# Top-k attention and two mixtures: how the first row tile passes the first mixture

## The chip, the cores and the metric

The kernel runs on one core of a Trainium2 chip. The metric is the device time of one execution in microseconds (us); three runs of the kernel before took 1279.56, 1282.32 and 1282.41 us, a median of 1282.32.

## The reference, cut to what matters

```python
# attention: 2 batches, 8 heads, 576 tokens, head size 64
scores = q @ k^T / 8
kth = the 32nd largest score of each row
attn = softmax(where(scores >= kth, scores, -1e9))
x = (attn @ v), heads side by side            # 1152 rows x 512
# first mixture: 512 -> 2048 -> 512
h = x @ w_in
x = (h * sigmoid(h)) @ w_out
# second mixture: 8 experts, 512 -> 1024 -> 512, Sinkhorn-normalised gates P (1152 x 8)
for e in range(8):
    out += P[:, e:e+1] * (maximum(x @ w1[e], 0) @ w2[e])
```

All inputs are drawn in double precision; `w_in` and `w_out` (and the other arrays) lie in DRAM as 8-byte words where they are double, and the kernel makes 4-byte floats of `w_in` and `w_out` itself.

## The kernel before, in words

The 1152 rows of x are nine row tiles of 128. Row tile 0 alone is group 0; tiles 1 and 2, 3 and 4, 5 and 6, 7 and 8 are groups 1 to 4. A group's attention is done in four units, one for each pair of heads; the unit of head pair p makes the 128 columns of chunk p of x. A score tile is 128 rows of scores against 576 keys: TensorE multiplies (L296), ScalarE copies the scores out of PSUM (L299), VectorE finds the 32 largest by four MAX8 and three MATCH_REPLACE (L308, L314), ScalarE takes the exponential (L312), VectorE masks and sums (L317), GpSimd adds 1e-9 (L319), VectorE takes the reciprocal (L320), ScalarE scales (L321), TensorE turns the tile (L324, L326), ScalarE copies it out (L337, L338), and TensorE multiplies by v into `pav` (L334). For group 0 the result goes into `x0` (L373).

Row tile 0 goes on first (`row_ffn` with the name m0, L497): for each of four column blocks F of 512 hidden columns, four products with the chunks of x0 (L515) into `banks[2]`, a tanh on ScalarE (L523), a multiply on VectorE that makes `gr` (L524), four turns (L531), a copy (L534), and, one block later, four products with `w_out` (L505) into `banks[0]`. Each 32-bit product of 128 by 512 columns shows as two records in the trace. The result becomes row tile 0 of `x1` (`x1_tile`, L584 to L593), and from there TensorE has other work than attention at any time: row tile 0 of experts 0 to 5 (`FILL`), then group 1's first mixture, and so on.

`w_in` and `w_out` come as 32 blocks of 128 by 512 double words (`first_blocks`, L454). Each block is loaded (L473) and narrowed (`narrow`, L439): ScalarE makes the upper bits (L445), GpSimd a correction `cv_n` from the lower word (L448), VectorE joins them (L452). The raw blocks rotate through four buffers, `cv_n` through five. The order of the blocks is by F: four of `w_in`, then four of `w_out`, four times. After the last load the 32 narrowed blocks are written to DRAM (L480) for the later groups.

The keys of a pair of heads are split into an upper and a lower part before they are turned: ScalarE copies (L214), GpSimd subtracts (L215), TensorE turns both (L219, L223), ScalarE copies out (L220, L225). All turns of keys and queries share one PSUM buffer.

Each engine runs its instructions in one order, which a scheduler writes when the program is built. It is steered by `tc.cur_priority`: lower numbers go first. All DMAs are issued by SyncE (SP), one after the other; where one has to wait, those behind it wait too.

Of the kernel before, what the change touches and what calls it, by code (L numbers as in the profile page):

```python
# [35 lines left out]
CVN = 5  # L36
# [12 lines left out]
NATURAL = True  # L49
EARLY_W = 0  # L50


def conv_at(i):

    return 11 * GAP + i * GAP * 2 // 32

# [8 lines left out]
def topk_attention_moe_sinkhorn_kernel(  # L65
# [128 lines left out]
    def load_kv(b, p):  # L194
        kn = nat.tile([P, 5, 2, 1 + NATURAL, D], F32, name=f"kn_{b}_{p}", tag="kn")
        vn = kvp.tile([P, 2, 5, D], F32, name=f"vn_{b}_{p}", tag="vn")
        ks, vs = (x[b, 2 * p : 2 * p + 2] for x in (k, v))
        for j in range(2):
            nc.sync.dma_start(kn[:, 0:4, j, 0, :], ks[j, 0 : 4 * P, :].rearrange("(p c) d -> p c d", c=4))
        nc.sync.dma_start(kn[0:64, 4, :, 0, :], ks[:, 4 * P : S, :].rearrange("h p d -> p h d"))  # L200
# [5 lines left out]
        return kn, vn  # L206

    def turn_kv(b, p, kn, vn):

        kk = kvp.tile([P, 2, S], F32R, name=f"kk_{b}_{p}", tag="kk")  # L210
        if NATURAL:
# [16 lines left out]
        def evac(cols, ps):  # L228
            for j in range(2):
                r, o = (slice(i * 64, (i + 1) * 64) for i in (j, 1 - j))  # L230
                nc.scalar.activation(kk[r, j, cols], ps[r], AF.Copy)
                nc.vector.tensor_sub(kk[o, j, cols], ps[r], kk[r, j, cols].bitcast(F32))

        pk = ps_p.tile([P, 4, P], F32, name=f"pk_{b}_{p}", tag="pp")
        for c in range(4):
            nc.tensor.transpose(pk[:, c, :], kn[:, c, :, 0, :].rearrange("p h d -> p (h d)"), ident)
        evac(slice(0, 512), pk.rearrange("p c t -> p (c t)"))
        pk2 = ps_p.tile([P, 64], F32, name=f"pk2_{b}_{p}", tag="pp")
        nc.tensor.transpose(pk2, kn[0:64, 4, :, 0, :].rearrange("p h d -> p (h d)"), ident[0:64, 0:64])
        evac(slice(512, S), pk2)  # L240
# [14 lines left out]
    def turn_q(b, p, t0, n, half, qn):  # L255
# [14 lines left out]
        pq = ps_p.tile([P, 2, 2 * P], F32, name=f"pq_{b}_{p}_{t0}", tag="pp")  # L270
# [18 lines left out]
    def score_tile(nm, qq, qL, kk, heads, cols):  # L289
# [29 lines left out]
        tiny.tensor_scalar(sm[:, 2:3], sm[:, 1:2], 1e-9, None, op0=ALU.add)  # L319
# [24 lines left out]
    def load(unit):  # L344
        g, p, b, t0, n, half, o = unit
        new = (b, p) not in kv
        if new:
            kv[b, p] = load_kv(b, p)
        return new, load_q(b, p, t0, n, half)

    def turn(unit, got):
        g, p, b, t0, n, half, o = unit
        if got[0]:
            kv[b, p] = turn_kv(b, p, *kv[b, p])
        return turn_q(b, p, t0, n, half, got[1])
# [83 lines left out]
    def narrow(x, src, i):  # L439
# [8 lines left out]
        nc.gpsimd.tensor_scalar(n, lo.bitcast(U32), 2.0**-32 * 7.49, None, op0=ALU.mult)  # L448
# [5 lines left out]
    def first_blocks():  # L454
# [5 lines left out]
        for i in (*range(15, nb), *reversed(range(15))):  # L460
            got[i] = cvp.tile([P, W], F32, name=f"wf_{i}", tag=f"wf{i}", bufs=1)
        for i in range(nb):
            tc.cur_priority = conv_at(i)
            F, part, c = i // (2 * NDC), i // NDC % 2, i % NDC
            r = slice(c * P, (c + 1) * P) if part == 0 else slice((F * NDC + c) * P, (F * NDC + c + 1) * P)
            cols = slice(F * W, (F + 1) * W) if part == 0 else slice(0, W)
            x = got[i]
            if w_in.dtype == F32:
                loaded = nc.sync.dma_start(x, (w_in, w_out)[part][r, cols])
            else:  # L470
                raw = cvp.tile([P, W], w_in.dtype, name=f"wfr_{i}", tag="raw")
                tc.cur_priority = 0 if i < EARLY_W else conv_at(i)
                loaded = (nc.scalar if i < EARLY_W else nc.sync).dma_start(raw, (w_in, w_out)[part][r, cols])  # L473
# [7 lines left out]
        return lambda F: [[got[(2 * F + part) * NDC + c] for c in range(NDC)] for part in range(2)]  # L481
# [15 lines left out]
    def row_ffn(nm, xF, y, gT_ps, blocks, nF, silu, pool):  # L497
# [10 lines left out]
        for F in range(nF):  # L508
            a, b = blocks(F)
            ph = banks[2]  # L510
            for c in range(NDC):
                if type(xF) is tuple:
                    mm3(ph, xF[0][:, c, :], xF[1][:, c, :], a[c][:, 0:W], a[c][:, W:], c == 0, c == NDC - 1)
                else:
                    nc.tensor.matmul(ph, xF[:, c, :], a[c], start=c == 0, stop=c == NDC - 1)  # L515
            kept = tc.cur_priority
            tc.cur_priority = uid() * 100
            g = x1p.tile([P, W], F32, name=f"gr_{nm}_{F}", tag="x1") if silu and NATURAL else \
                pool.tile([P, W], F32, name=f"gr_{nm}_{F}", tag="g")
            if silu:  # L520

                t = pool.tile([P, W], F32, name=f"tr_{nm}_{F}", tag="t")
                nc.scalar.activation(t, ph, AF.Tanh, scale=0.5)  # L523
                nc.vector.scalar_tensor_tensor(g, t, 1.0, ph, op0=ALU.add, op1=ALU.mult)  # L524
            else:
                nc.scalar.activation(g, ph, AF.Relu)
# [118 lines left out]
    qs = turn(units[0], got[0])  # L645
    for u, unit in enumerate(units):
# [19 lines left out]
        if g == 0:  # L666
# [3 lines left out]
            row_ffn("m0", x0, banks[0], banks[1], blocks, DFF // W, True, hp0)  # L670
# [343 lines left out]
```

## Time and profile before

| | us |
|---|---|
| median of three runs | 1282.32 |
| the profiled execution | 1280.4 |
| its span, first to last instruction | 1278.5 |
| TensorE busy | 1201.5 (94%) |
| VectorE busy | 815.7 (64%) |

The page's slices show VectorE at nine tenths or more from the second slice to the fifteenth (a slice is 32 us), and TensorE at nine tenths or more from the sixth to the end, after 4, 5, 6 and 8 tenths. To read the profile: a stretch of the span is taken by itself, the engine that is never idle in it is looked up, and then what the other engines wait for there. The row "TensorE's clock" (PEclk) is the granted share of 2.4 GHz; 0.50 is 1.2 GHz.

### The profile page before, as it was taken

The numbers are of one execution on the slowest core, as the hardware profiler recorded it, in microseconds if no ns is written. First come the engines' busy times: TensorE is split into PE (matmuls) and PEld (weight loads), VectorE is DVE, ScalarE is ACT, GpSimd is POOL, SyncE is SP. The second block draws the span as 40 slices with busy tenths as digits, with TensorE's granted clock in tenths as the row PEclk, the third lists the DMA queues.
The fourth block names the chain that finished last, engine by engine and source line by source line (L and its number), as shares of the span: only waits on it lengthen the run. The fifth ranks groups of instructions, "written<-read, shape, count | busy, mean of one in ns | idle before, by whom it ended". The sixth has DMA issues, their size and how long they took to land.

```text
span 1278.5 us, 17534 instructions
## 1 busy us (share of the span) xinstructions
PE 1201.5 (94%) x6035; PEld 950.3 (74%) x6035; DVE 815.7 (64%) x1531; ACT 580.8 (45%) x1132; POOL 572.8 (45%) x645
## 2 busy tenths in 40 slices
PE   4568999999999999999898999999999999999998
PEld 3444666678767778888676888888888888888887
DVE  4999999989999999132455543454534445354343
ACT  5665777777776577322312332232332322233221
POOL 7971476767751274220233443353444433344310
PEclk9868999999999999999998999999999999999999
DMA  8776576799867689775432312131121111211001
GB/s 235 224 240 226 177 238 221 251 351 323 291 231 246 216 298 326 248 248 181 154 110 82 91 50 66 34 91 42 34 73 43 58 46 45 66 36 56 25 1 66
DMA packets 126538, 193.07 MB, mean 151 GB/s; under 512 B 22896, under 2 KB 68976, under 8 KB 126448
## 3 DMA queue, kind: packets, MB, share of 16 engines
q1 hardware_dynamic: 126448, 191.94, 45.8%
q8 instruction: 48, 0.79, 0.3%
q14 instruction: 42, 0.34, 0.1%
HBM read 152.85 MB, written 39.06 MB: 150 GB/s over the span
## 4 chain that ended last, share of the span: by engine, by line
PE 68%; DVE 25%; DMA 2%; ACT 2%; issue 1%; POOL 1%; DVEq 0%; SPq 0%; POOLq 0%; ACTq 0%
DVE m L308 9%; PE h L140 9%; PE h L138 9%; PE h L139 8%; DVE w L314 7%; PE yA L140 4%; PE yA L139 4%; PE yA L138 4%; PE yB L138 4%; PE yB L139 4%; PE yB L140 4%; DVE s L317 3%; PE bank L138 3%; PE bank L139 3%; PE bank L140 3%; PE bank L505 2%
## 5 line engine op out<-in xcount | busy, mean ns | idle before, releaser
L130 POOL TENSOR_TENSOR wp<-rw,wp 128x512 fp32r<-128x512 f32 (+1 forms) x56 | 86.7, 1571 | 207.8 <-ACT wp L129 207.8
L308 DVE MAX8 m<-w 128x8 f32<-128x576 f32 x192 | 139.3, 743 | 0.3
L130 POOL TENSOR_TENSOR wa<-raw,wa 128x512 fp32r<-128x512 f32 x88 | 116.7, 1337 | 36.3 <-ACT wa L129 29.1
L130 POOL TENSOR_TENSOR w<-rw,w 128x512 fp32r<-128x512 f32 x56 | 73.1, 1308 | 107.4 <-ACT w L129 107.4
L314 DVE MATCH_REPLACE8 w<-m,w 128x576 f32<-128x576 f32 x128 | 94.3, 738 | 0.0
L138 PE MATMUL yB<-w,gH_0b 128*128 128x512 f32 x208 | 81.0, 390 | 0.0
L139 PE MATMUL yB<-w,gH_0b 128*128 128x512 f32 x208 | 81.0, 389 | 0.0
L865 DVE SCALAR_TENSOR_TENSOR gL_0b<-gB,gH_0b 128x512 fp32r<-128x512 f32 (+1 forms) x56 | 45.0, 803 | 55.3 <-ACT gH_0b L864 54.5
L140 PE MATMUL yB<-w,gL_0b 128*128 128x512 f32 x208 | 80.2, 390 | 0.0
L317 DVE SCALAR_TENSOR_TENSOR s<-s,m,e 128x576 f32<-128x576 f32 x64 | 68.9, 1077 | 0.3
L864 ACT ACTIVATE gH_0b<-gB 128x512 fp32r<-128x512 f32 (+1 forms) x56 | 33.6, 600 | 76.5 <-PE yB L139 43.5
L138 PE MATMUL h<-x1H,wp 128*128 128x512 f32 x168 | 67.0, 399 | 0.1
L140 PE MATMUL h<-x1H,wp 128*128 128x512 f32 x168 | 67.0, 399 | 0.0
L139 PE MATMUL h<-x1L,wp 128*128 128x512 f32 x168 | 66.8, 397 | 0.0
L321 ACT ACTIVATE s<-s,sm 128x576 f32<-128x576 f32 x64 | 49.7, 779 | 32.0 <-DVE sm L320 31.6
L312 ACT ACTIVATE e<-s,sm 128x576 f32<-128x576 f32 x64 | 50.0, 781 | 30.1 <-DVE s L317 18.6
L878 DVE TENSOR_TENSOR gB<-u,h 128x512 f32<-128x512 f32 x56 | 38.5, 688 | 37.4 <-PE h L140 37.3
L129 ACT ACTIVATE w<-rw 128x512 fp32r<-128x512 f32 x56 | 34.7, 627 | 58.9 <-PE yB L140 45.7
L505 PE MATMUL bank<-wb,gT_e 128*128 128x512 f32 x128 | 58.8, 599 | 1.7 <-ACT gT_e L534 1.7
L130 DVE TENSOR_TENSOR wp<-sp,wp 128x1024 fp32r<-128x1024 f32 x28 | 44.7, 1596 | 20.2 <-ACT wp L129 20.2
L324 PE MATMUL pt<-ident,s 128*128 128x128 f32 x256 | 43.6, 297 | 13.6 <-ACT s L321 12.7
L334 PE MATMUL pav<-aT,vn 128*64 128x256 f32 (+3 forms) x480 | 53.3, 354 | 2.9 <-ACT aT L337 2.5
(348 smaller groups left out, 3645.6 us busy)
## 6 DMA issues: line engine op xcount, KB each, us to landing
rw<-in_moe_w_dram SPq DMA_DIRECT2D x112, 256.0 KB, 2.7
wa<-sk SPq DMA_DIRECT2D x48, 512.0 KB, 4.1
wb<-sk SPq DMA_DIRECT2D x48, 512.0 KB, 4.3
raw<-in_moe_w_dram SPq DMA_DIRECT2D x80, 256.0 KB, 4.1
wb<-in_moe_w_dram SPq DMA_DIRECT2D x32, 512.0 KB, 5.2
sk<-wa SPq DMA_DIRECT2D x24, 512.0 KB, 4.2
sk<-wb SPq DMA_DIRECT2D x24, 512.0 KB, 4.2
wfr<-in_moe_w_in_dram SPq DMA_DIRECT2D x16, 512.0 KB, 4.6
```

The source lines that it names most:

```text
L130: eng.tensor_sub(dL, src, dH.bitcast(F32))
L138: nc.tensor.matmul(ps, wH, xH, start=first, stop=False, skip_group_check=more)
L139: nc.tensor.matmul(ps, wH, xL, start=False, stop=False, skip_group_check=more)
L140: nc.tensor.matmul(ps, wL, xH, start=False, stop=last, skip_group_check=more)
L308: nc.vector.max(mr, src)
L312: nc.scalar.activation(e, s, AF.Exp, scale=SCALE, bias=sm[:, 0:1])
L314: nc.vector.match_replace(out=w, in_to_replace=mr, in_values=src, imm_value=-3e38)
L317: nc.vector.scalar_tensor_tensor(s, s, m8[:, TOPK - 1 : TOPK], e, op0=ALU.is_ge, op1=ALU.mult, accum_out=sm[:, 1:2])
L321: nc.scalar.activation(s, s, AF.Copy, scale=sm[:, 3:4])
L334: nc.tensor.matmul(ps[r, :n], vn[:, j, c, :], aT[j][:, c, :n], start=c == 0, stop=c == 4)
L505: nc.tensor.matmul(y, gT[:, c * P : (c + 1) * P], b[c], start=F == 0 and c == 0, stop=F == nF - 1 and c == NDC - 1)
L865: nc.vector.scalar_tensor_tensor(gL, src, 0.0, gH.bitcast(F32), op0=ALU.max, op1=ALU.subtract)
```

## The change

Five things change.

1. In `first_row`, which takes the place of `row_ffn` for row tile 0 of the first mixture, blocks F = 0, 1 and 2 are summed side by side in three PSUM banks, one product for each as soon as a chunk of x0 is there. F = 3 follows when bank 2 is free. Turns and second products come after.
2. The 32 blocks are narrowed in another order: all 16 of `w_in` by chunk, then the 16 of `w_out`. The first six raw loads get an earlier priority.
3. Every third `cv_n` is made by ScalarE in place of GpSimd; `cv_n` has four buffers in place of five.
4. The first unit's keys are turned as they are; upper and lower part are made when they leave PSUM, by ScalarE and VectorE (what the code had under `NATURAL = False`), and the first unit's turns use free banks in place of the shared buffer.
5. The loads of v get a later priority than those of k and q.

```diff
-CVN = 5
+CVN = 4
...
-NATURAL = True
-EARLY_W = 0
+V_LATE = GAP
+SOON = 6
+ON_ACT = 3
...
-        def evac(cols, ps):
-            for j in range(2):
-                r, o = (slice(i * 64, (i + 1) * 64) for i in (j, 1 - j))
-                nc.scalar.activation(kk[r, j, cols], ps[r], AF.Copy)
-                nc.vector.tensor_sub(kk[o, j, cols], ps[r], kk[r, j, cols].bitcast(F32))
+        def evac(j, cols, ps):
+            r, o = (slice(i * 64, (i + 1) * 64) for i in (j, 1 - j))
+            nc.scalar.activation(kk[r, j, cols], ps[r], AF.Copy)
+            nc.vector.tensor_sub(kk[o, j, cols], ps[r], kk[r, j, cols].bitcast(F32))
...
+        pk2 = banks[0][:, 0:64]
+        nc.tensor.transpose(pk2, kn[0:64, 4, 0, :, :].rearrange("p h d -> p (h d)"), ident[0:64, 0:64])
...
+        pq = banks[1].rearrange("p (a b) -> p a b", a=2) if first else \
+            ps_p.tile([P, 2, 2 * P], F32, name=f"pq_{b}_{p}_{t0}", tag="pp")
...
+        if new:
+            kept = tc.cur_priority
+            tc.cur_priority += V_LATE
+            load_v(b, p, kv[b, p][1])
+            tc.cur_priority = kept
...
-        nc.gpsimd.tensor_scalar(n, lo.bitcast(U32), 2.0**-32 * 7.49, None, op0=ALU.mult)
+        if ON_ACT and i % ON_ACT == ON_ACT - 1:
+            nc.scalar.activation(n, lo.bitcast(U32), AF.Copy, scale=2.0**-32 * 7.49)
+        else:
+            nc.gpsimd.tensor_scalar(n, lo.bitcast(U32), 2.0**-32 * 7.49, None, op0=ALU.mult)
...
+        order = [(0, F, c) for c in range(NDC) for F in range(DFF // W)] + \
+            [(1, F, c) for F in range(DFF // W) for c in range(NDC)]
...
+    def first_row(xF, got, pool):
...
+        y, gT_ps = banks[0], banks[1]
+        ph = [banks[2], banks[1], banks[0]] + [banks[2]] * (nF - 3)
...
+        for c in range(NDC):
+            for F in range(3):
+                hide(F, c)
+        silu(0)
+        silu(1)
+        turned(0)
+        silu(2)
+        for F in range(3, nF):
+            for c in range(NDC):
+                hide(F, c)
+            turned(1)
+            silu(F)
+        for F in range(nF):
+            second(F)
+            if F + 2 < nF:
+                turned(F + 2)
```

TensorE at the start of the program, before: `pk` are turned keys, `pq` turned queries, `ps` scores; names end with unit and tile.

```order
L219 MATMUL pk_0_0_156<-ident,kn_0_131 128x128 x4
L219 MATMUL pk_0_1_162<-ident,kn_0_131 128x128 x4
L223 MATMUL pk_0_0_168<-ident,kn_0_131 128x64 x2
L273 MATMUL pq_0_0_174<-ident,qd_0_0_172 128x128 x2
L296 MATMUL ps_0_0_0_0_223<-kk_0_151,qq_0_0_177 128x288 x2
L219 MATMUL pk_1_0_196<-ident,kn_1_141 128x128 x4
L296 MATMUL ps_0_0_0_0_223<-kk_0_151,qL_0_0_178 128x288 x2
```

The same place now:

```order
L245 MATMUL pk_0_152<-ident,kn_0_131 128x128 x4
L247 MATMUL bank_128<-ident,kn_0_131 128x64
L287 MATMUL bank_129<-ident,qd_0_0_166 128x128 x2
L310 MATMUL ps_0_0_0_0_216<-kk_0_151,qq_0_0_170 128x288 x2
L310 MATMUL ps_0_0_0_0_216<-kk_0_151,qL_0_0_171 128x288 x2
L229 MATMUL pk_1_0_189<-ident,kn_1_141 128x128 x4
```

Five turns of keys stand where ten stood, each in a place of its own, and the second unit's turn no longer stands between the two halves of the first score tile.

TensorE after the last chunk of x0, before: the products of F = 0 with the last chunk, then those of F = 1 between the turns of F = 0.

```order
L515 MATMUL bank_130<-wf_660,x_86 128x512
L531 MATMUL bank_129<-ident,gr_m_0_892 128x128
L515 MATMUL bank_130<-wf_655,x_86 128x512
L531 MATMUL bank_129<-ident,gr_m_0_892 128x128
L515 MATMUL bank_130<-wf_654,x_86 128x512
L531 MATMUL bank_129<-ident,gr_m_0_892 128x128
L515 MATMUL bank_130<-wf_653,x_86 128x512
L531 MATMUL bank_129<-ident,gr_m_0_892 128x128
L515 MATMUL bank_130<-wf_652,x_86 128x512
```

The same place now (three such products also stand after each of the three earlier chunks):

```order
L516 MATMUL bank_130<-wf_653,x_86 128x512
L516 MATMUL bank_129<-wf_654,x_86 128x512
L516 MATMUL bank_128<-wf_655,x_86 128x512
L337 MATMUL pt_0_0_0_0_1628<-ident,s_0_0_0_0_1609 128x128 x4
L339 MATMUL pt_1_0_0_0_0_1633<-ident,s_0_0_0_0_1609 128x128
L516 MATMUL bank_130<-wf_644,x_86 128x512
L516 MATMUL bank_130<-wf_648,x_86 128x512
L516 MATMUL bank_130<-wf_652,x_86 128x512
L516 MATMUL bank_130<-wf_656,x_86 128x512
```

Seven first products are left after the last chunk in place of thirteen (the other eight of before stand further on, in two blocks of four).

VectorE up to the reciprocal that row tile 0's last score tile needs, before:

```order
L452 SCALAR_TENSOR_TENSOR wf_638<-wf_638,cv_n_793 128x512
L314 MATCH_REPLACE w_0_0_0_0_1618<-m_1_0_0_0_0_1619,w_0_0_0_0_1618 128x576
L308 MAX m_1_0_0_1_0_1685<-s_0_0_1_0_1682 128x8
L134 TENSOR_TENSOR qL_2_1_1766<-pq_2_1_1760,qq_2_1_1765 128x512
L452 SCALAR_TENSOR_TENSOR wf_639<-wf_639,cv_n_799 128x512
L320 RECIPROCAL sm_0_3_0_0_560<-sm_0_3_0_0_560 128x1
L308 MAX m_1_0_0_0_1_1652<-w_0_0_0_1_1651 128x8
L308 MAX m_1_0_0_0_0_1619<-w_0_0_0_0_1618 128x8
L452 SCALAR_TENSOR_TENSOR wf_640<-wf_640,cv_n_805 128x512
L314 MATCH_REPLACE w_0_0_0_1_1651<-m_1_0_0_0_1_1652,w_0_0_0_1_1651 128x576
L452 SCALAR_TENSOR_TENSOR wf_641<-wf_641,cv_n_811 128x512
L320 RECIPROCAL sm_0_3_1_0_593<-sm_0_3_1_0_593 128x1
```

The same place now:

```order
L474 SCALAR_TENSOR_TENSOR wf_625<-wf_625,cv_n_846 128x512
L333 RECIPROCAL sm_0_3_0_0_553<-sm_0_3_0_0_553 128x1
L321 MAX m_0_0_3_1_0_585<-w_0_3_1_0_584 128x8
L140 TENSOR_TENSOR qL_2_1_1759<-pq_2_1_1753,qq_2_1_1758 128x512
L327 MATCH_REPLACE w_0_0_0_0_1611<-m_1_0_0_0_0_1612,w_0_0_0_0_1611 128x576
L330 SCALAR_TENSOR_TENSOR s_0_3_1_0_582,sm_0_3_1_0_586<-s_0_3_1_0_582,m_0_0_3_1_0_585,e_0_3_1_0_587 128x576
L327 MATCH_REPLACE w_0_0_0_1_1644<-m_1_0_0_0_1_1645,s_0_0_0_1_1642 128x576
L321 MAX m_1_0_0_0_0_1612<-w_0_0_0_0_1611 128x8
L321 MAX m_1_0_0_1_1_1711<-s_0_0_1_1_1708 128x8
L321 MAX m_1_0_0_0_1_1645<-w_0_0_0_1_1644 128x8
L333 RECIPROCAL sm_0_3_1_0_586<-sm_0_3_1_0_586 128x1
```

`wf_625` is the last of the 32 blocks: all narrowing now stands ahead of this reciprocal, where 25 of 32 did.

## Rows read from the trace of the kernel before

**Rows 1.** Stretches of the span: length, busy us (instructions) of each engine, TensorE's clock, DMA
```profile
core 0: us, PE busy (x) PEld busy (x) DVE busy (x) ACT busy (x) POOL busy (x), PEclk, DMA share, GB/s
51.50:97.10 45.60, 26.23 (x134) 18.74 (x132) 45.60 (x96) 27.53 (x53) 35.72 (x38) 0.67 0.73 238
97.10:144.60 47.50, 40.97 (x166) 22.89 (x165) 47.50 (x107) 26.46 (x50) 5.43 (x17) 0.92 0.48 173
144.60:512.30 367.70, 355.46 (x2135) 270.08 (x2136) 357.29 (x787) 275.56 (x591) 221.06 (x287) 1.00 0.80 272
512.30:522.00 9.70, 9.70 (x72) 7.90 (x71) 0.40 (x1) 4.13 (x12) 1.84 (x3) 1.00 0.94 328
```
**Rows 2.** Timeline of the first unit: start, us, engine, line, operation, count, [idle before]
```profile
4.66 1.28 ACT L214 ACT_TABLE_LOAD   x1 [4.66 <-DMA kn<-in_k_dram]
6.67 1.67 POOL L215 TENSOR_TENSOR kn<-kn 128x512 f32<-128x512 f32 x2 [3.53 <-ACT kn L214]
7.98 1.11 PE L219 MATMUL pk<-ident,kn 128*128 128x128 f32 x4 [7.98 <-POOL kn L215]
12.58 0.66 PE L273 MATMUL pq<-ident,qd 128*128 128x128 f32 x2 [0.46 <-POOL qd L268]
13.71 0.85 PE L296 MATMUL ps<-kk,qq 128*128 128x288 f32 x2 [0.47 <-ACT qq L133]
16.62 0.76 DVE L308 MAX8 m<-s 128x8 f32<-128x576 f32 x1 [2.51 <-ACT s L299]
```
**Rows 3.** Timeline of VectorE: last reciprocal of row tile 0, first multiply, x1's lower part
```profile
90.59 0.15 DVE L320 RECIPROCAL sm<-sm 128x1 f32<-128x1 f32 x1
...
103.06 0.67 DVE L524 SCALAR_TENSOR_TENSOR gr_m<-tr_m,bank 128x512 f32<-128x512 f32 x1
...
146.68 0.67 DVE L134 TENSOR_TENSOR x1L<-bank,x1H 128x512 fp32r<-128x512 f32 x1
```
**Rows 4.** Line 452 by itself: durations min/median/max in ns, first and last start
```profile
L452 DVE SCALAR_TENSOR_TENSOR wf<-wf,cv_n x32: 665/676/1704, 17.3 to 105.7; 128x512 int32<-128x512 int32 x32
```
**Rows 5.** Timeline of TensorE: the first mixture of row tile 0, to expert 0
```profile
51.58 1.81 PE L515 MATMUL bank<-wf,x 128*128 128x512 f32 x2
...
97.19 1.28 PE L515 MATMUL bank<-wf,x 128*128 128x512 f32 x2
103.79 0.47 PE L531 MATMUL bank<-ident,gr_m 128*128 128x128 f32 x1 [5.32 <-DVE gr_m L524]
104.06 1.92 PE L515 MATMUL bank<-wf,x 128*128 128x512 f32 x2
...
107.84 1.02 PE L515 MATMUL bank<-wf,x 128*128 128x512 f32 x2
...
110.22 3.60 PE L505 MATMUL bank<-wf,gT_m 128*128 128x512 f32 x8
...
144.64 0.50 PE L138 MATMUL bank<-wa,x1H 128*128 128x512 f32 x1 [0.26 <-ACT x1H L133]
```
**Rows 6.** Waits of SP's queue from 40 to 175 us: total, times, longest
```profile
SPq L247 <- POOL qd L268: 25.3, 4, 24.2
SPq L473 <- POOL cv_n L448: 16.7, 12, 3.3
SPq L473 <- ACT wf L445: 12.1, 7, 3.8
```
**Rows 7.** Line 448 by itself, as in rows 4
```profile
L448 POOL TENSOR_SCALAR cv_n<-wfr x32: 1515/1543/2127, 14.8 to 97.9; 128x512 int32<-128x512 uint32 x32
```
**Rows 8.** Timeline of VectorE and TensorE where attention ends
```profile
511.33 0.16 DVE L320 RECIPROCAL sm<-sm 128x1 f32<-128x1 f32 x1 [0.33 <-POOL sm L319]
...
515.27 0.60 PE L324 MATMUL pt<-ident,s 128*128 128x128 f32 x4
...
518.73 2.38 PE L334 MATMUL pav<-aT,vn 128*64 128x256 f32 x20
```

More of the change, by code (lines that the diff above doesn't have):

```diff
@@ L253, in load_q, with turn_q @@
         return qn
-    def turn_q(b, p, t0, n, half, qn):
+    def turn_q(b, p, t0, n, half, qn, first=False):
         w = n * P
@@ L318, in score_tile @@
                                        accum_out=sm[:, 1:2])
[L319 removed]
+        nc.gpsimd.tensor_scalar(sm[:, 2:3], sm[:, 1:2], 1e-9, None, op0=ALU.add)
         nc.vector.reciprocal(sm[:, 3:4], sm[:, 2:3])
@@ L347, in load, with turn @@
         if new:
-            kv[b, p] = load_kv(b, p)
-        return new, load_q(b, p, t0, n, half)
-    def turn(unit, got):
+            kv[b, p] = load_kv(b, p, not kv)
+        qn = load_q(b, p, t0, n, half)
+        if new:
+            kept = tc.cur_priority
+            tc.cur_priority += V_LATE
+            load_v(b, p, kv[b, p][1])
+            tc.cur_priority = kept
+        return new, qn
+    def turn(unit, got, first=False):
         g, p, b, t0, n, half, o = unit
         if got[0]:
-            kv[b, p] = turn_kv(b, p, *kv[b, p])
-        return turn_q(b, p, t0, n, half, got[1])
+            kv[b, p] = turn_kv(b, p, *kv[b, p], first)
+        return turn_q(b, p, t0, n, half, got[1], first)
     def tiles(unit, qs, xH, xL):
@@ L459, in first_blocks @@
         got, writes = {}, []
-        for i in (*range(15, nb), *reversed(range(15))):
-            got[i] = cvp.tile([P, W], F32, name=f"wf_{i}", tag=f"wf{i}", bufs=1)
-        for i in range(nb):
+        order = [(0, F, c) for c in range(NDC) for F in range(DFF // W)] + \
+            [(1, F, c) for F in range(DFF // W) for c in range(NDC)]
+        for i in rooms(nb):
+            part, F, c = order[i]
+            got[part, F, c] = cvp.tile([P, W], F32, name=f"wf_{i}", tag=f"wf{i}", bufs=1)
+        for i, (part, F, c) in enumerate(order):
             tc.cur_priority = conv_at(i)
-            F, part, c = i // (2 * NDC), i // NDC % 2, i % NDC
             r = slice(c * P, (c + 1) * P) if part == 0 else slice((F * NDC + c) * P, (F * NDC + c + 1) * P)
             cols = slice(F * W, (F + 1) * W) if part == 0 else slice(0, W)
-            x = got[i]
+            x = got[part, F, c]
             if w_in.dtype == F32:
@@ L511, in row_ffn @@
             for c in range(NDC):
[L512 to L515, printed above, removed]
+                mm3(ph, xF[0][:, c, :], xF[1][:, c, :], a[c][:, 0:W], a[c][:, W:], c == 0, c == NDC - 1)
             kept = tc.cur_priority
             tc.cur_priority = uid() * 100
[L518 to L526, printed above, removed]
+            g = pool.tile([P, W], F32, name=f"gr_{nm}_{F}", tag="g")
+            nc.scalar.activation(g, ph, AF.Relu)
             tc.cur_priority = kept
@@ L644, in topk_attention_moe_sinkhorn_kernel @@
     got = {0: load(units[0]), 1: load(units[1])}
-    qs = turn(units[0], got[0])
+    qs = turn(units[0], got[0], True)
     for u, unit in enumerate(units):
```

72 lines of the change are left out of this document (50 added, 22 removed).

## The prediction

> **What bounds the kernel now.** I read the page's slices first: after 160 us TensorE is at nine tenths or more to the end, while VectorE is full only until about 510 us. Whatever shortens this kernel must therefore let TensorE start its long run of work earlier, or take waits or work out of that run. Then I cut the span into stretches with their busy times [rows 1]. From 144.6 to 512.3 us TensorE is busy 355.5 of 367.7 us, so 12.2 us of idle are all there is to win in that stretch; from 512.3 to 522 us it is busy 9.70 of 9.70. Up to 97.1 us it is different: 26.2 of 45.6 us busy, at a granted clock of 0.67, so at 1.2 GHz in much of it, while VectorE is busy in all 45.6. Between 97.1 us (the last chunk of x0 is there) and 144.6 us (expert 0 starts) both engines are nearly full: TensorE 41.0 of 47.5, VectorE 47.5 of 47.5. So two things set when the long run starts: VectorE's work up to x0, and the chain of TensorE from x0 to expert 0. The change touches both.
>
> After the timelines of the first unit [rows 2] I read VectorE around x0 [rows 3], the narrowing [rows 4, 7], TensorE's chain [rows 5], and SP's waits [rows 6]. All sums below are against the profiled execution (1280.4 us, span 1278.5), which lies 1.9 us under the median of the three runs, 1282.3; they are put on that median at the end.
>
> **1. The first unit.** Before, keys landed at 4.66 us; then came a table load of 1.28, ScalarE's copy, GpSimd's subtraction until 8.3, turns from 7.98, turned queries at 12.58, scores at 13.71, and the first MAX8 at 16.62 [rows 2]. Now the turn needs no copy and no subtraction. Landing at 4.7, turns of 1.1 to 5.8, ScalarE's copy 0.6 and VectorE's subtraction 0.6 to about 7.2 (each bounded by the 0.67 that a 128x512 subtraction from PSUM takes [rows 3]). The table load stands first on ScalarE with no wait ahead of it, so it is over by then. Queries are issued third in place of sixth on SP and are turned by 7.5; ScalarE does the next pair's copy ahead of the query copy, which puts the scores at about 8.2. From the scores to the MAX8 took 2.91 us with the second pair's turn in between; without that turn I take 2.7, so MAX8 at about 10.9: 5.7 us earlier. Bounds: 4 (the second pair's keys land late and hold up ScalarE) and 7.
>
> **2. VectorE up to x0.** Its order decides here, since it is never idle from 51.5 to 144.6 us [rows 1]. Ahead of the last reciprocal of row tile 0 stood 25 of 32 narrowings, now 32: seven more at the median of 676 ns [rows 4] are 4.7 us. The first unit's four subtractions (about 1.5 us) stand ahead of the first MAX8 in the order and are over when the scores come, so they add nothing behind it. VectorE starts 5.7 us earlier and has 4.7 more to do: 90.59 becomes about 89.6. x0 is hardly earlier, but the narrowing is over by then.
>
> **3. Products moved ahead of x0.** Six products (F = 1 and 2, chunks 0 to 2) move in front of 97.1 us. One took 1.81 us there at the low clock [rows 5], so 10.9 us go into a stretch with 45.6 - 26.2 = 19.4 us of idle [rows 1]: TensorE itself has room. But each burst of three, 5.4 us, now stands between score tiles of the next units and the last turns, and scores that come late hold VectorE up. There was one product in each of these places. Bounds: 0, if the score tiles are made far enough ahead, and 8, if each of three bursts holds VectorE for 2.7 us, half its length; I take 3, since VectorE had no idle there though a product of 1.81 stood in the same places, so there is some slack. Cost: +3 us, which reaches x0.
>
> The Trainium skill says on the page TensorE: Matmul & The Clock Gate, Part 1, What's actually happening, that "the default state is throttled, and activity releases the throttle". The trace agrees on the way down and up: 0.67 in the half-idle stretch, 1.92 us for a product at 104.06 after a wait of 5.32 and 1.02 at 107.84 after steady work [rows 1, 5]. By that rule the added products might lift the clock ahead of x0; whether they are enough no row shows. If they did, the bursts would take about 3 us each, the cost of this part would be 0, and the time 3 us lower, which is the first rival below.
>
> **4. From x0 to expert 0.** Before: 47.5 us, 6.5 of it idle, of which 5.32 us waited for VectorE's first multiply [rows 1, 5]. Thirteen first products stood in it, now seven: six fewer at 0.9 us (3.60 for four, measured on the second products [rows 5]) are -5.4. Low clock: before, about 2.7 us were lost to it (one product at 1.28, two at 1.92 in place of 0.9 [rows 5]); now the three products of the last chunk meet it, about 2.9 lost. These cancel. The wait: the multiply came 12.5 us after the last reciprocal [rows 3]; now 16 instructions stand between them, none a narrowing, about 10.1 us by the same durations. The three last products run until about 9 to 12 us after the reciprocal, so TensorE waits 0 to 1.5 us for the multiply before F = 3; I take 0.7, which is -4.6. The second products and turns are the same in number. Together -9.8 us, with bounds of -5 (three more waits of the chain show, since F = 3 goes through the same bank and the turns through one other) and -12. Some attention (ten turns and four score products, about 2.5 us) falls behind the start of expert 0 in the new order; it is moved, not saved, and not counted.
>
> The expert's weights must come earlier too. Before, SP sat 24.2 us behind a load of queries that waited for GpSimd's copy [rows 6], which waited for a turn on TensorE; the weights were issued behind it, 6.4 us ahead of expert 0's first product. In the new order that turn stands ahead of eight second products (7.2 us) and the last turns, so the weights arrive in time, by some 5 us.
>
> **5. After that.** TensorE's work is the same in amount, its 12.2 us of waits I leave as they are (bounds -4 and +4). VectorE's attention would end about 3 to 6 us earlier than 511.3; TensorE came to the last tile 4 us later [rows 8], and has a few experts' products left. In the new order these stand ahead of the last score tile, so nothing covers the copies between its turn and `pav`, and then the step to the next mixture: +1 us, 0 to 2.5.
>
> Sum: -5.7 + 4.7 + 3 - 9.8 + 1 = -6.8, so 1273.6 on the profiled execution and 1275.5 on the median. The moves to ScalarE (ten corrections) and the later loads of v I cost at nothing: ScalarE was busy 27.5 of 45.6 us in the stretch, and GpSimd, which loses them, 35.7 [rows 1]; without that cover the narrowing would be later, which is the last rival.
>
> **Rivals.** *A. The clock or the slack pays for the bursts.* Part 3 costs 0 and the chain gives 11, since its first products meet less of the low clock: -5.7 + 4.7 - 11 + 1 = -11, 1271 on the median. For it: 19.4 us of idle. Against: the clock there was low with 26 us of work. Chance 0.2.
>
> *B. x0 comes later and takes the gain.* Each of three bursts holds VectorE for 2.7, cost 8: sum -1.8, about 1280.5. For it: VectorE has no idle, so what it waits there is lost. Against: its order was made with five buffers of scores to work ahead. Chance 0.22.
>
> *C. Slower: the narrowing isn't ready in time.* VectorE takes instructions in order, and all 32 narrowings now stand ahead of the last reciprocal. Before, the last correction started at 97.9 us [rows 7]. If loads and GpSimd go no faster, the last narrowing cannot start before 99.5, the reciprocal follows ten instructions later at about 105, 14.4 us late, and x0 with it: with -9.8 and +1 this gives +5.6, 1288. It decides from a delay of x0 of 9 us. For it: 16.8 MB of raw words must land some 12 us earlier. Against: the loads mostly waited for corrections, 16.7 us, and for ScalarE, 12.1 [rows 6], not for the DMA (share 0.73 [rows 1]), and GpSimd gives up ten corrections of 1.5 us and the first pair's subtractions. Chance 0.13.
>
> **How the numbers follow.** The forecast holds 0.45 (its own range 1272 to 1280), A 0.2, B 0.22, C 0.13. A measurement can tell 0.3%, 3.8 us, from no change; so faster is under 1278.5. That takes all of A and about 0.9 of the forecast, 0.6; the same takes the rest of the forecast and 0.85 of B, 0.24; slower is C and the tail of B, 0.16. The range goes from 1266 (A with the bounds of parts 1 and 5) to 1285, which takes in B with a bound of part 5 and leaves out most of C.
>
> **What would show it.** Right: first MAX8 near 11 us; the last reciprocal of row tile 0 between 89 and 95; seven first products after x0; expert 0's first product at 135 to 139 in place of 144.6; idle of TensorE from there to 520 us still near 12 us. Wrong: VectorE waits for corrections or for scores before 90 us; GpSimd or SP delays expert 0's weights; or TensorE's start comes earlier but the idle between 145 and 520 us grows by as much, which would mean that VectorE's end of attention sets the end of the run.

## The result, and the profile after

| | before | changed |
|---|---|---|
| median of four runs, us | 1281.24 | 1263.07 |
| range, us | 1279.56 to 1282.41 | 1262.10 to 1265.75 |
| span of the profiled execution, us | 1278.5 | 1261.9 |

The ratio is 0.9862, 95% interval [0.9841, 0.9884]. A second set of runs of the same kernel, with its own runs of before beside it, gave 1265.42 us and 0.9881 [0.9867, 0.9894]. So the change saves 15 to 18 us; 6.8 were forecast, and the time lies below the range of 1266 to 1285.

The first fence has stretches of the changed kernel's span, cut at its own milestones: from the first MAX8 to the last reciprocal of row tile 0, from the last chunk of x0 to expert 0, and from there to the end. Columns as in [rows 1].

```profile
11.74:88.75 77.01, 46.78 (x209) 33.16 (x209) 76.91 (x154) 57.52 (x110) 56.08 (x64) 0.76 0.93 310
95.02:129.20 34.18, 32.15 (x136) 17.84 (x135) 34.18 (x76) 21.13 (x40) 5.38 (x14) 0.99 0.38 125
129.20:1261.90 1132.70, 1104.25 (x5642) 888.06 (x5642) 697.79 (x1286) 500.64 (x976) 488.96 (x537) 0.99 0.44 142
```

The numbers behind the length of a stretch are busy times: TensorE's products, its weight loads, VectorE, ScalarE, GpSimd. VectorE is idle for 0.1 of the first 77 us. The second stretch answers to 47.5 us in [rows 1]: TensorE is idle for 2.0 us in it instead of 6.5. The third was 1133.9 us long before. The page's chain of waits moved with it: VectorE's share of it is 19%, in before 25%; TensorE's is 77%, in before 68%.

Timelines of the changed kernel, VectorE, answering to [rows 2, 3]:

```profile
11.74 0.76 DVE L321 MAX8 m<-s 128x8 f32<-128x576 f32 x1 [2.15 <-ACT s L313]
...
88.75 0.14 DVE L333 RECIPROCAL sm<-sm 128x1 f32<-128x1 f32 x1
...
98.73 0.67 DVE L524 SCALAR_TENSOR_TENSOR gr_m<-tr_m,bank 128x512 f32<-128x512 f32 x1
...
131.02 0.67 DVE L140 TENSOR_TENSOR x1L<-bank,x1H 128x512 fp32r<-128x512 f32 x1
```

and TensorE, answering to [rows 5] (a product is two records):

```profile
62.68 2.84 PE L516 MATMUL bank<-wf,x 128*128 128x512 f32 x6 [0.19 <-ACT x L392]
...
81.51 3.05 PE L516 MATMUL bank<-wf,x 128*128 128x512 f32 x6
...
95.02 3.12 PE L516 MATMUL bank<-wf,x 128*128 128x512 f32 x6
...
99.46 3.70 PE L516 MATMUL bank<-wf,x 128*128 128x512 f32 x8 [0.77 <-DVE gr_m L524]
...
106.94 3.70 PE L538 MATMUL bank<-wf,gT_m 128*128 128x512 f32 x8 [0.38 <-DVE gr_m L524]
...
129.20 0.50 PE L144 MATMUL bank<-wa,x1H 128*128 128x512 f32 x1 [0.24 <-ACT x1H L139]
```

Bursts of three products take 2.84 to 3.12 us, 0.95 to 1.04 for a product. The mean clock ahead of x0 did not rise with them: from 51.5 us to the last chunk of x0 it is 0.66, in before 0.67 [rows 1]. The wait for the first multiply is 0.77 us instead of 5.32. Expert 0 starts 15.4 us earlier.

The narrowing on VectorE, and then the corrections on GpSimd, each line by itself (min/median/max in ns, first and last start), answering to [rows 4, 7]:

```profile
L474 DVE SCALAR_TENSOR_TENSOR wf<-wf,cv_n x32: 666/678/1753, 14.1 to 82.7; 128x512 int32<-128x512 int32 x32
```

```profile
L470 POOL TENSOR_SCALAR cv_n<-wfr x22: 1521/1538/2072, 10.4 to 78.2; 128x512 int32<-128x512 uint32 x22
```

The last correction starts at 78.2 instead of 97.9. SP's waits from 40 to 175 us, answering to [rows 6]: those of the raw loads (L498) for corrections are down from 16.7 us to 11.8, and it still sits 20.0 us behind one load of queries. Expert 0's first product does not show it: it waits 0.24 us, and for x1H, not for weights (last row above).

```profile
SPq L260 <- POOL qd L281: 24.0, 3, 20.0
...
SPq L498 <- ACT cv_n L468: 6.3, 4, 2.0
SPq L498 <- POOL cv_n L470: 5.5, 4, 2.0
```

Where attention ends, against [rows 8], the last reciprocal is only 2.3 us earlier, while expert 0 started 15.4 us earlier:

```profile
509.07 0.16 DVE L333 RECIPROCAL sm<-sm 128x1 f32<-128x1 f32 x1 [0.33 <-POOL sm L332]
```

By the steps of the prediction, on the profiled executions (the last column has the two numbers that each step is the difference of):

| step | forecast | measured | from |
|---|---|---|---|
| 1, first MAX8 | -5.7 | -4.9 | 16.62, 11.74 |
| 2, VectorE to the last reciprocal | +4.7 | +3.0 | 73.97, 77.01 |
| 3, bursts hold VectorE | +3 | 0 | 0.1 idle of 77.01 |
| reciprocal to last chunk | 0 | -0.3 | 6.60, 6.27 |
| 4, last chunk to expert 0 | -9.8 | -13.3 | 47.45, 34.18 |
| 5, expert 0 to the end | +1 | -1.2 | 1133.9, 1132.7 |
| sum | -6.8 | -16.6 | 1278.5, 1261.9 |

In the trace of the second set, against the same trace of before, the steps are -4.6, +3.6, 0, -0.3, -13.3 and +0.7, together -13.8. So steps 1 to 4 come again to within 0.7 us, and the last one, -1.2 or +0.7, says nothing against the forecast of +1.

### The profile page after: what moved, and what is told of

It reads as the page before. It is cut to its first block, busy times and chain, and to the rows that moved or that the text cites. A ratio compares the mean times of both kernels' runs of the same rounds, so it can differ in the third digit from the quotient of the medians.

```text
span 1261.9 us, 17508 instructions
## 1 busy us (share of the span) xinstructions
PE 1192.4 (94%) x6030; PEld 946.0 (75%) x6030; DVE 817.2 (65%) x1535; ACT 588.2 (47%) x1141; POOL 557.0 (44%) x633
## 4 chain that ended last, share of the span: by engine, by line
PE 77%; DVE 19%; DMA 1%; ACT 1%; issue 1%; SPq 0%; POOL 0%; DVEq 0%; ACTq 0%
PE h L144 9%; PE h L146 9%; PE h L145 9%; DVE m L321 6%; DVE w L327 5%; PE bank L144 4%; PE bank L145 4%; PE bank L580 4%; PE bank L146 4%; PE yB L145 4%; PE yB L144 4%; PE yA L146 4%; PE yA L145 4%; PE yB L146 4%; PE yA L144 4%; PE pav L347 2%
## 5 line engine op out<-in xcount | busy, mean ns | idle before, releaser
L337 PEld LDWEIGHTS pt<-ident,s 128*128 128x128 f32 x256 | 31.6, 147 | 32.9 <-ACT s L334 23.8
```

What stands on the lines that cost most here:

```text
L337: nc.tensor.transpose(pt[:, c, :], s[:, c * P : (c + 1) * P], ident)
```

## The experiments

Ten kernels ran, one of them twice, and the changed kernel once more, in three sets, each on one chip with runs of the kernel before beside it (1281.13, 1280.27 and 1280.71 us). The milestones (us) are read from each kernel's trace as above. The changed kernel's own two sets differ by 2.3 us of time and 1.9 us after expert 0, so differences of that size between kernels of different sets show nothing.

| kernel | last reciprocal | expert 0 | from there to the end | median | ratio, interval |
|---|---|---|---|---|---|
| before | 90.6 | 144.6 | 1133.9 | 1281.2 | 1 |
| changed | 88.8 | 129.2 | 1132.7 | 1263.1 | 0.9862 [0.9841, 0.9884] |
| changed, second set | 89.7 | 130.1 | 1134.6 | 1265.4 | 0.9881 [0.9867, 0.9894] |
| first unit undone | 91.1 | 128.1 | 1136.0 | 1266.5 | 0.9886 [0.9871, 0.9901] |
| chain block by block | 88.0 | 139.5 | 1130.1 | 1271.1 | 0.9925 [0.9908, 0.9942] |
| bursts twice | 90.8 | 133.4 | 1131.5 | 1266.8 | 0.9892 [0.9877, 0.9907] |
| blocks by F | 90.1 | 130.5 | 1132.9 | 1265.3 | 0.9880 [0.9866, 0.9895] |
| narrowing alone | 95.2 | 143.7 | 1131.5 | 1277.0 | 0.9973 [0.9963, 0.9982] |
| first unit alone | 81.8 | 133.6 | 1140.1 | 1274.2 | 0.9953 [0.9938, 0.9968] |
| corrections on GpSimd | 82.6 | 123.2 | 1134.6 | 1260.5 | 0.9839 [0.9825, 0.9854] |
| the same, second set | 82.7 | 123.3 | 1134.7 | 1260.1 | 0.9839 [0.9825, 0.9852] |
| GpSimd, late loads | 81.0 | 122.8 | 1139.0 | 1263.1 | 0.9857 [0.9838, 0.9877] |
| every fifth on ScalarE | 86.4 | 124.6 | 1140.4 | 1266.9 | 0.9896 [0.9881, 0.9911] |
| ScalarE for w_out only | 84.1 | 124.1 | 1138.0 | 1262.7 | 0.9861 [0.9848, 0.9875] |

**The chain as before.**

```diff
-        for c in range(NDC):
-            for F in range(3):
-                hide(F, c)
...
+        for F in range(nF):
+            for c in range(NDC):
+                hide(F, c)
+            silu(F)
+            if F:
+                second(F - 1)
+            turned(F)
+        second(nF - 1)
```

> The changed kernel with only the chain of row tile 0 as in the kernel before: block after block through one bank, thirteen first products behind the last chunk of x0 in place of seven; narrowing, first unit and loads as changed. Theory (most of the gain is this chain: six products of 0.86 us, 4.5 us less waiting for VectorE's first multiply, about 2 us of low clock): last reciprocal of row tile 0 within 1.5 us of 88.75, TensorE waits some 5 us for the first multiply, expert 0 starts near 140 in place of 129.2, time 10 us longer (8 to 13). Rival 1 (the gain is the earlier and cheaper x0 and what else moved in the order): time at most 4 us longer. Rival 2 (the bursts cost x0 something): reciprocal 3 us earlier without them, near 85.5, time 7 us longer.

Reciprocal and expert 0 came as the theory had them; the time is 5.7 to 8.0 us longer than in the changed kernel's two sets, at and below the low end of 8 to 13. The wait of 5 us did not come. TensorE between the last chunk of x0 and expert 0, groups by line (count, busy us, mean ns, idle before), in this kernel

```profile
L516 PE MATMUL bank<-wf,x 128*128 128x512 f32 x26 | 11.8, 594 | 0.0
...
L529 PE MATMUL bank<-ident,gr_m 128*128 128x128 f32 x16 | 2.5, 279 | 1.5 <-DVE gr_m L524 1.5
```

in the kernel before

```profile
L515 PE MATMUL bank<-wf,x 128*128 128x512 f32 x26 | 14.3, 675 | 0.1
...
L531 PE MATMUL bank<-ident,gr_m 128*128 128x128 f32 x16 | 3.4, 302 | 5.3 <-DVE gr_m L524 5.3
```

and in the changed one

```profile
L516 PE MATMUL bank<-wf,x 128*128 128x512 f32 x14 | 6.8, 627 | 0.8 <-DVE gr_m L524 0.8
L337 PE MATMUL pt<-ident,s 128*128 128x128 f32 x24 | 3.7, 275 | 0.0
```

With the same 26 records, the low clock is gone (11.8 instead of 14.3 us, granted clock 1.00 instead of 0.92) and most of the wait for the multiply too (5.3 to 1.5 us; all idle of TensorE in the stretch, 6.5 to 4.0, since 1.3 us of waiting for a score copy came in). So 2.5 us of clock and 2.5 of idle were not won by the new chain. The chain itself gives the next step: 11.8 to 6.8, less waiting (4.0 idle to 2.0, all causes), and fewer attention instructions in the shorter time. The whole stretch is 47.5, 44.1 and 34.2 us long in the three kernels, so 9.9 of its 13.3 us are the chain's.

What broke up the long wait is work that stands in it. VectorE makes 5 narrowings between the last reciprocal and the multiply in before, none in this kernel; TensorE has nothing between the last chunk of x0 and the multiply's turns in before, and in this kernel the turns of one score tile and the products of another. Two kernels below come out the same way: "narrowing alone" has no narrowing there, the attention work, and a wait of 0.44 us, "first unit alone" 4 narrowings, no such work, and a wait of 3.74, with nearly the same time from reciprocal to multiply (9.9 and 10.0 us). That the attention work is ready there because VectorE is free of narrowings is argued from these orders, not shown by a run.

**Bursts twice.**

```diff
+            for F in range(3 if c < NDC - 1 else 0):
+                nc.tensor.matmul(ph[F], xF[:, c, :], got[0, F, c], start=False, stop=False)
```

> The changed kernel with each of the first three bursts done twice: the nine first products of chunks 0 to 2 with F = 0, 1 and 2 are added a second time into the same banks, so row tile 0 is computed from other sums. Nine products of about 0.95 us more stand ahead of x0 on TensorE. Theory (TensorE has slack there, VectorE works ahead by its buffers of scores, the bursts cost x0 nothing): last reciprocal of row tile 0 between 87 and 89.5, no wait of VectorE after its first MAX8, time within 1.5 us of the changed kernel's. Rival (bursts hold VectorE up, as part 3 of the prediction had it, 1 us for each): VectorE waits for scores ahead of 88 us, reciprocal at 91 to 94, time 3 to 5 us longer.

Between the two. VectorE's waits from its first MAX8 to the last reciprocal (us, times, longest):

```profile
DVE m L321 <- ACT s L313: 2.9, 2, 2.4
DVE wf L474 <- ACT cv_n L468: 1.2, 3, 0.6
DVE qL L140 <- ACT qq L139: 0.2, 1, 0.2
```

The one of 2.4 is the first MAX8's own, which the changed kernel has too; the other 1.9 us are new, 1.2 of them for corrections that ScalarE makes and only 0.5 for scores. The reciprocal is 1.2 to 2.1 us later and the last chunk 4.8 to 5.7: the third double burst runs from 90.0 to 96.3 us, across the reciprocal at 90.8 and ahead of the last turns for x0. A burst of three fits the slack, one of six does not.

**First unit undone, and alone.**

```diff
-            kv[b, p] = load_kv(b, p, not kv)
+            kv[b, p] = load_kv(b, p)
...
-    qs = turn(units[0], got[0], True)
+    qs = turn(units[0], got[0])
```

> The changed kernel with its first unit as in the kernel before: keys split ahead of the turns, all turns through the one shared buffer. The first MAX8 should go back from 11.7 us to about 16.6. Theory (VectorE never waits between its first MAX8 and the last reciprocal of row tile 0, so its order alone sets that time): the order of this kernel has four narrowings ahead of the first MAX8 and 28 behind it, so 4.9 us of later start are paid with 4 x 0.75 = 3.0 us of work that is already done, and two instructions fewer stand ahead: last reciprocal near 90 in place of 88.75, the time 1 us longer (0 to 2.5). Rival 1 (the earlier first MAX8 goes through to the end in full): reciprocal near 93.6, time 4.9 us longer. Rival 2 (x0 is set by the narrowing, not by the start): no change at all, reciprocal within 0.3 us.

The first MAX8 went to 17.48, the reciprocal only to 91.1: the rival of a full 4.9 us falls, for four narrowings fill the time ahead of the MAX8. Expert 0 even starts 1.1 us earlier, and the later stretch is 3.3 us longer. The time is 3.4 us over the changed kernel's first set and 1.0 over its second.

"Alone" keeps the new first unit and has the chain as before (the diff above), the blocks in the old order (the diff under "blocks by F" below), and:

```diff
-V_LATE = GAP
-SOON = 6
-ON_ACT = 3
+V_LATE = 0
+SOON = 0
+ON_ACT = 0
```

> The kernel before with only its first unit changed (keys turned as they are, turns in free banks), beside that four correction buffers in place of five; narrowing order, GpSimd's corrections, loads and the chain of row tile 0 as before. Theory (the order of VectorE sets x0; here 21 narrowings stand ahead of the last reciprocal, in before 25): first MAX8 near 11.8, reciprocal near 82 to 84 in place of 90.6, expert 0's first product near 133 in place of 144.6, time 11 us shorter than before, near 1270 (1267 to 1273). Rival 1 (only the 4.9 us of the earlier first MAX8 arrive): time 5 us shorter, near 1276. Rival 2 (as the removal of the first unit from the changed kernel has it, which cost 2 to 3 us): time 1278.

Reciprocal 81.8 and expert 0 at 133.6, as the theory said; the time is 6.1 us shorter than before, not 11 (nearer to the first rival's 5), for the stretch after expert 0 is 6.2 us longer. The wait came back, and the low clock with it:

```profile
92.51 1.11 PE L528 MATMUL bank<-ident,gr_m 128*128 128x128 f32 x4 [3.74 <-DVE gr_m L523]
93.42 5.64 PE L515 MATMUL bank<-wf,x 128*128 128x512 f32 x8
```

5.64 us for four products; the next four take 3.60.

**Narrowing alone:** the first unit and the chain of before (their diffs are above), and no early or late loads.

```diff
-V_LATE = GAP
-SOON = 6
+V_LATE = 0
+SOON = 0
```

> The kernel before with only the narrowing changed (w_in by chunk ahead of w_out, every third correction on ScalarE, four correction buffers); the first unit, the loads and the chain of row tile 0 as before. Theory (the order of VectorE sets x0 and the chain; the end is expert 0's start plus 1130 to 1133 us plus half of the low clock in it): first MAX8 near 17, last reciprocal of row tile 0 near 92.5, no narrowing between it and the first multiply, x1's lower part near 142.5 in place of 146.7, time 4 us shorter than before (2 to 7), so near 1277. Rival 1 (this part brings all of the gain that is not the chain's): time 9 to 10 us shorter than before. Rival 2 (seven more narrowings ahead of x0 are a pure cost when nothing else is changed): time 3 us longer than before.

3.3 us shorter, as the theory said, but not by its x0: the last chunk came 4.3 us later than before (101.47), as step 2 had it. From there to expert 0 it is 42.2 us instead of 47.5. The turns of a score tile and score products stand ahead of the multiply's turns, and the first multiply is waited for no longer than this:

```profile
102.58 0.66 PE L337 MATMUL pt<-ident,s 128*128 128x128 f32 x4
...
104.63 0.54 PE L310 MATMUL ps<-kk,qq 128*128 128x288 f32 x2 [1.29 <-ACT s L313]
...
105.87 0.66 PE L529 MATMUL bank<-ident,gr_m 128*128 128x128 f32 x4 [0.44 <-DVE gr_m L524]
106.36 3.60 PE L516 MATMUL bank<-wf,x 128*128 128x512 f32 x8
```

**Blocks by F.**

```diff
-        order = [(0, F, c) for c in range(NDC) for F in range(DFF // W)] + \
-            [(1, F, c) for F in range(DFF // W) for c in range(NDC)]
+        order = [(part, F, c) for F in range(DFF // W) for part in range(2) for c in range(NDC)]
```

> The changed kernel with the 32 blocks narrowed in the old order (by F, four of w_in and four of w_out in turn), all else as changed. VectorE's order up to x0 is the same row by row. Theory (what counts is how many narrowings stand ahead of x0, not which; the twelfth block of w_in for F = 0 to 2 is the 20th of the old order and narrowed near 60 us, before the last two bursts ask for it): last reciprocal of row tile 0 within 1 us of 88.75, expert 0 within 1 us of 129.2, time within 2 us of the changed kernel's 1263. Rival (w_in has to be ahead of w_out for the bursts): a burst waits for VectorE, scores behind it come late, reciprocal 3 us later or more, time 3 us longer or more.

No difference from the changed kernel's second set (1265.3 and 1265.4). That w_in goes ahead of w_out does nothing here: both have 32 narrowings ahead of the last reciprocal.

**Where the corrections are made.** With ON_ACT = n ScalarE makes every n-th correction, with 0 none; SOON is how many raw loads are issued early (6 in the changed kernel, 0 is "late loads"). ON_ACT = 0:

> The changed kernel with all 32 corrections on GpSimd again, none on ScalarE. Theory (VectorE's order up to x0 sets x0, and the end follows x0 and the chain): 23 narrowings stand ahead of the last reciprocal in place of 32, nine of 0.75 us less, and each of the 23 costs some 0.07 us more with a busier GpSimd (0.82 before against 0.75 after): reciprocal near 84 in place of 88.75, expert 0's first product near 124 in place of 129.2, time 4 to 5 us shorter. Rival 1 (the last narrowings of w_out, now on VectorE behind the first multiplies, come late for the second products, or GpSimd splits expert 0's weights late): expert 0 starts no earlier than 129, time the same or up to 5 us longer, and TensorE waits more than 3 us between the last chunk of x0 and expert 0. Rival 2 (GpSimd holds VectorE up): narrowings of 0.9 us and more, reciprocal at 88 or later, time 2 us longer or more.

ON_ACT = 0 and SOON = 0:

> The changed kernel with all corrections on GpSimd and without the earlier priority of the first six raw loads: 22 narrowings stand ahead of the last reciprocal of row tile 0 in place of 32 (23 with GpSimd's corrections alone). Theory (each narrowing moved behind x0 is time won, as long as the second products don't wait for it): reciprocal near 81 in place of 88.75, expert 0 near 122, time 1259 to 1261, at or below that of GpSimd's corrections alone (1260.5). Rival (what is moved behind x0 comes back in the chain): expert 0 at 126 or later, time 1263 or more.

The last set, on one chip: the changed kernel, ON_ACT = 0, ON_ACT = 5, and `if i >= 16 and i % 3 == 2` for ScalarE's share.

> The changed kernel once more, beside the next three on one chip. Every theory: 1263 us, 18 us under the kernel before (17 to 19).

> The changed kernel with all corrections on GpSimd, once more, to compare it on one chip with the changed kernel. Theory (x0 comes 6 us earlier, about 2 to 4 of them reach the end): 2 to 4 us below the changed kernel. Rival (what was seen was a difference between two chips or sets of runs): within 1 us of it.

> The changed kernel with every fifth correction on ScalarE in place of every third: 30 narrowings ahead of the last reciprocal of row tile 0 in place of 32, and by the order six instructions of row tile 0 and of the next units fewer up to x1's lower part. Theory (the sum of VectorE's order up to there sets expert 0's start): reciprocal near 86 in place of 88.75, expert 0 near 124 in place of 129.2; between nothing and 3 us of it are given back later, so 1258 to 1261. Rival (only the narrowings ahead of x0 count, two of 0.75 us): expert 0 near 127.7, time 1261 to 1263.

> The changed kernel with ScalarE's share of the corrections (every third) only among the 16 blocks of w_out: 27 narrowings ahead of the last reciprocal in place of 32. Theory: reciprocal near 83.5, expert 0 near 123.5; up to 3 us given back later, so 1258 to 1261, the same as with all corrections on GpSimd. Rival (w_in late: the corrections of w_in are GpSimd's alone, and a burst waits for its blocks): VectorE waits for scores ahead of x0, reciprocal at 86 or later, time 1263 or more.

The changed kernel's second set missed what was expected of it: 15.3 us under the kernel before, not 17 to 19.

With all corrections on GpSimd the kernel is 5.3 us faster than the changed one on the same chip, and the two intervals don't meet: the third edit of the change, ScalarE's share, costs time. The narrowings up to the last reciprocal, in the second set of the GpSimd kernel

```profile
L474 DVE SCALAR_TENSOR_TENSOR wf<-wf,cv_n 128x512 int32<-128x512 int32 x23 | 17.2, 748 | 0.0
```

and in the changed kernel's second set

```profile
L474 DVE SCALAR_TENSOR_TENSOR wf<-wf,cv_n 128x512 int32<-128x512 int32 x32 | 24.2, 770 | 0.0
```

7.0 us fewer ahead of x0, and expert 0 at 123.3 instead of 130.1. In all four GpSimd-heavy kernels (0, 0 with late loads, every fifth, w_out only) the theory gave expert 0's start to within 1 us. It failed for the time of three, which are 3 to 8 us longer after expert 0 than the changed kernel and the first GpSimd kernel: late loads, every fifth and w_out only. For ON_ACT = 0 itself the gain was 2.5 us against the changed kernel's first set, where 4 to 5 were expected, and 5.3 beside its second, where 2 to 4 were. "Late loads" waited 3.5 us on VectorE ahead of the reciprocal, 3.4 of it for corrections, and still had x0 early. TensorE's longest waits after expert 0 up to the end of attention, with every fifth on ScalarE:

```profile
PE bank L144 <- DVE g_m L430: 6.4, 6, 2.6
PE ps L310 <- ACT s L313: 3.2, 5, 1.0
PE bank L596 <- ACT gr_e L591: 2.4, 1, 2.4
```

and in the changed kernel:

```profile
PE pt L337 <- ACT s L334: 3.4, 4, 1.4
PE pav L347 <- ACT aT L350: 2.6, 2, 2.0
PE bank L144 <- DVE g_m L430: 2.3, 3, 1.2
```

From expert 0 to the end TensorE is idle for 28.5 us in the changed kernel, 33.5 with late loads and 34.6 with every fifth: there what is given back is idle of TensorE, in the rows above for the mixtures' multiplies and for score copies. With w_out only it is idle for 29.1 us and busy for 4.6 us more. Why one order of VectorE gives back more than another is open.

The later loads of v and the four buffers in place of five were not tried alone.

## Why the prediction was wrong

The direction and the places were right, the size was not. Done alone, the parts add up: first unit alone -6.1, narrowing alone -3.3, both with the loads -10.0 (the kernel with the old chain), and the chain on top of that -6 to -8. Undone they do not: taking the first unit out of the changed kernel costs 1.0 to 3.4 us, not 6.1.

*Step 1* held in kind: -4.9 at the first MAX8 for -5.7. The scores' products began at 8.16 us, as forecast; what was left out is that the early raw loads put a narrowing's work on ScalarE ahead of the first score copy, which waits behind it for a raw block. ScalarE in the changed kernel:

```profile
10.38 0.66 ACT L464 ACTIVATE wf<-wfr 128x512 f32<-128x512 f32 x1 [1.07 <-DMA wfr<-in_moe_w_in_dram]
11.06 0.65 ACT L313 ACTIVATE s<-ps 128x576 f32<-128x576 f32 x1
```

and with late loads:

```profile
9.30 0.65 ACT L313 ACTIVATE s<-ps 128x576 f32<-128x576 f32 x1 [0.22 <-PE ps L310]
```

With the new first unit and no early loads (late loads, first unit alone) the first MAX8 starts at 9.9 to 10.0 us, with early loads at 11.5 to 12.1 in every kernel.

*Step 2* held in kind. Seven more narrowings cost 3.0 us (3.6 in the second set), not 4.7, for the 25 of before had taken longer. Up to the last reciprocal, before:

```profile
L452 DVE SCALAR_TENSOR_TENSOR wf<-wf,cv_n 128x512 int32<-128x512 int32 x25 | 20.5, 821 | 0.0
```

and after:

```profile
L474 DVE SCALAR_TENSOR_TENSOR wf<-wf,cv_n 128x512 int32<-128x512 int32 x32 | 23.6, 752 | 0.0
```

The median of [rows 4] was near 676 in both; the mean was not. That the moves to ScalarE cost nothing, as the sum took it, was wrong: they are why 32 and not 23 narrowings stand ahead of x0.

*Step 3* is the first that failed: +3 forecast, nothing measured. The price of 1.81 us for a product was the first of three, in [rows 5]; the two others of the same kind in the trace of before took 1.02:

```profile
70.50 1.02 PE L515 MATMUL bank<-wf,x 128*128 128x512 f32 x2
...
81.95 1.02 PE L515 MATMUL bank<-wf,x 128*128 128x512 f32 x2
```

A burst was 2.84 to 3.12 us, not 5.4. Rival A, at 0.2, named this. Its clock did not rise ahead of x0 (0.66, in before 0.67): two of the three products of before had been quick already. The doubled bursts show that the slack was real and about one burst wide.

*Step 4* failed in size, and it is the largest term: -13.3 for -9.8. The multiply's wait went as forecast (5.32 to 0.77; the forecast had 0.7). "These cancel" was the error: the low clock was to cost as much as before, and it was gone. First products went from 14.3 to 6.8 us of busy time, 7.5 where six of 0.9 make 5.4. The kernel with the old chain and the one with narrowing alone show that the low clock went with the long wait and not with the fewer products: where TensorE waits 5.3 or 3.7 us for the multiply (before, first unit alone) the granted clock from the last chunk to expert 0 is 0.92 and 0.93, and where it waits 0.4 or 0.9 us (narrowing alone, old chain) it is 1.00, with the same thirteen first products. Not every wait was followed by it: the four products behind the late loads' wait of 2.88 us took 3.70.

```profile
93.32 3.70 PE L516 MATMUL bank<-wf,x 128*128 128x512 f32 x8 [2.88 <-DVE gr_m L524]
```

The Trainium skill, page TensorE: Matmul & The Clock Gate, Part 1, What's actually happening, states that "activity releases the throttle"; the rows agree here, 1.92 us for a product after the long wait in [rows 5] and 0.92 in the changed kernel's four at 99.46. The rest, some 1.4 us, is attention that moved behind expert 0, which the forecast named and left out of the term: 29 turns of scores stand in the stretch where 39 did, and 17 records of score products for 24.

*Step 5*: +1 forecast, -1.2 and +0.7 measured, within the bounds of -4 and +4 that were set for it. VectorE's attention ended 2.3 us earlier, not 3 to 6. The stretch from expert 0 to the end holds nearly the same work in every kernel here (5623 to 5650 records of TensorE), and it took 1130.1 to 1140.4 us. The forecast of "unchanged" fits the changed kernel and would have failed for "first unit alone" by 6.

*Rivals.* B and C did not come: VectorE did not wait, and the last correction began at 78.2. A was right that the bursts cost nothing and that the chain meets less of the low clock, and still 5.6 us short, by steps 2, 4 and 5. The signs that were listed came in part: MAX8 near 11 (11.74), seven first products after x0, idle near 12 later; the reciprocal came at 88.75, a little before 89 to 95, and expert 0 at 129.2, well before 135 to 139.

The errors of steps 2 to 5 all had one sign in this trace, and those of steps 2 to 4 in both, so the range, whose low end moved only parts 1 and 5 to their bounds, was too narrow on that side. Two small slips weigh little: the rows that the prediction names for the low clock of before give 2.4 us and not 2.7, and the page has TensorE at nine tenths from 128 us, not 160, with three later slices at eight.

**A better version** is the changed kernel with ON_ACT = 0: 1260.1 and 1260.5 us in two sets, 0.9839 of before, against 1263.1 and 1265.4. Of these, 1260.1 and 1265.4 were measured on one chip, and their intervals don't meet.

## What to carry to other kernels

Price a moved instruction by all its rows in the stretch, mean and longest, and not by the first or the median; and when a long wait goes, look whether a low clock followed it, and count that as gone too. A milestone behind an engine that is never idle comes earlier by what no longer stands ahead of it there, so moving helper work to a faster engine can cost time: here ten corrections on ScalarE put 32 narrowings ahead of x0 instead of 23. What an earlier start of the long stretch brings has to be measured: here that stretch came out between 3.8 us shorter and 6.5 us longer than before.

## What was not expected of the hardware

A narrowing takes 0.67 us, but the first one in the kernel before took 1.70: GpSimd had just begun to subtract the parts of the keys. Timeline of the kernel before, GpSimd and VectorE:

```profile
17.18 2.13 POOL L215 TENSOR_TENSOR kn<-kn 128x512 f32<-128x512 f32 x2 [0.88 <-ACT kn L214]
17.30 1.70 DVE L452 SCALAR_TENSOR_TENSOR wf<-wf,cv_n 128x512 int32<-128x512 int32 x1
...
22.42 3.73 POOL L448 TENSOR_SCALAR cv_n<-wfr 128x512 int32<-128x512 uint32 x2
24.09 0.67 DVE L452 SCALAR_TENSOR_TENSOR wf<-wf,cv_n 128x512 int32<-128x512 int32 x1
```

Another narrowing, which began 0.1 us ahead of such a subtraction, took 0.67:

```profile
37.81 0.67 DVE L452 SCALAR_TENSOR_TENSOR wf<-wf,cv_n 128x512 int32<-128x512 int32 x1
...
37.91 1.72 POOL L215 TENSOR_TENSOR kn<-kn 128x512 f32<-128x512 f32 x1
```

Beside a correction most narrowings are not slower: 15 of the 22 in that trace took under 0.72 us, the other seven 0.76 to 1.06. The Trainium skill, page SBUF — State Buffer, Who interferes with whom, states that a VectorE instruction with two SBUF inputs contends with a GpSimd instruction that reads SBUF. The trace agrees for GpSimd's two-input subtraction; for its one-input correction, which reads SBUF as well, it agrees at most in those seven, and what sets them apart is open.
